# Attention's last 64 queries in one TensorE group for the scores and one for the values, and the last 64 keys as a block-diagonal tile

## The chip, the core and the metric

The kernel runs on one core of a Trainium2 chip. TensorE (PE) multiplies, VectorE (DVE) and ScalarE (ACT) work element by element, GpSimd (POOL) fills constants, and SyncE (SP) issues the transfers. The metric is the device time of one execution in microseconds. Every duration below comes from one profiled execution of the kernel before.

## The reference

Eight batches with eight heads of 576 tokens go through causal attention with a decay, and then through a two-layer network with a gate:

```python
B, H, S, D = 8, 8, 576, 64
cum    = cumsum(log(clip(f, 1e-4, 1)), -1)
scores = q @ k.T / sqrt(D) + cum[..., :, None] - cum[..., None, :]
scores = where(causal, -1e9, scores)
attn   = softmax(scores)                 # exp(scores - max), over the sum + 1e-9
x      = (attn @ v).transpose(0, 2, 1, 3).reshape(B * S, H * D)   # 4608 x 512
h      = x @ w_in                        # 512 -> 2048
g      = h * tanh(softplus(h))           # the Mish function
out    = g @ w_out                       # 2048 -> 512
```

## The kernel before

**Two streams of work.** Attention goes by pairs of heads: 32 pairs `g`, four to a batch. The network (`m1_items`, `m2_items`) goes by chunks of 512 tokens and 16 steps of 128 hidden units; eight chunks hold the first 512 tokens of a batch each, the ninth holds the last 64 tokens of all batches. Each float32 matrix is split into two float16 halves, so a product of the network is three matmuls of 512 columns: `b<-xa,wall` for the first layer, `b<-gh,wall` and `b<-gl,wall` for the second. ACT computes Mish (tile `me`), ACT or DVE makes its high half `gh` and DVE the low half `gl`.

**Order.** Nothing is issued as written. `Program.choose` collects every operation with its possible engines and a price, and `schedule` plays the program forward on priced engines (with nine backward passes for the ranks) and writes out the order with the earliest modelled end. Each engine then runs its list in that order, and semaphores hold it where an operand is late. An item given to `choose` as a list of several operations is placed as one piece: nothing is put between its parts. `beside` does that for products that fill half of the array each.

**Attention of pairs 4 to 31** (28 pairs; the first four go another way, which the change does not touch). Queries stand on the partitions. A pair's 576 queries are four blocks of 128 and a last one of 64, and the last 64 queries of both heads share one tile: head 0 on partitions 0 to 63, head 1 on 64 to 127. The functions are nested in `attn_moe`:

- `new_st_items` makes scores in a PSUM bank (two products each: 70 rows of `st`, then 128), finds the row's highest (`highest`, DVE), and takes exponentials (`exp`, ACT) into `st` (buffer `ST1[2]`); `turn` splits them into halves `hb` and transposes them by a transfer into `pt`. Its part `w_` is that of the last 64 queries: against the last 64 keys (bank `pv`, "narrow", 64 columns) and the first 512 (bank `ps`, "wide", 512 columns), for both heads: eight products `b<-st` that fill 64 of the array's 128 columns. The narrow exponentials go to `ev` (128x64), then twice side by side into `hv` (128x128), and by a transposing transfer into `tv`.
- `new_pv_items` multiplies exponentials by values (`b<-vv,pt`): `blocks` for whole query blocks, and `tail` for the last 64 queries: for four key blocks three products per head, 24 of half width, and for the last 64 keys three per head from `tv`, which take 64 rows and 64 columns of the array each (64*64 in the rows below).

Attention's PSUM banks are two (`bank`), taken in turn; the network has the other six. In ACT, exponentials and Mish need different tables, so that ACT_TABLE_LOAD stands wherever the order goes from one to the other.

The price of an operation on PE is (columns, active columns, half); a further product in one `choose` way cost 53 columns:

```python
if isinstance(cost, tuple) and total:
    total = (total[0] + 53, total[1] + cost[1], 0)
```

Of the kernel before, what the change touches and what calls it, by code (L numbers as in the profile page):

```python
# [15 lines left out]
F32 = mybir.dt.float32  # L16
# [10 lines left out]
P = 128  # L27
S = 576
# [30 lines left out]
NME = 5  # L59
NOT = 2  # L60
NGH = 5
SPD = 0
WO0 = 16
LWO = 4
# [77 lines left out]
class Program:  # L142
# [21 lines left out]
    def choose(self, *ways):  # L164

        r, w, opts = [], [], []
        for way in ways:
            total, port = 0.0, False
            for eng, method, a, kw in way:
                aps = [(k, x) for k, x in list(enumerate(a)) + list(kw.items()) if hasattr(x, "tensor")]  # L170
                w += [z for k, x in aps if k in ("out", "accum_out", 0) for z in self.region(x)]
                r += [z for k, x in aps if k not in ("out", "accum_out", 0) for z in self.region(x)]
                if eng == "scalar":
                    (r if method == "activation" else w).append(("table", 0, 1, 0, 1))
                if eng == "tensor":

                    w.append((w[0][0] + "/pe", 0, 1, 0, 1))
                port |= self.shared(eng, method, aps)
                cost = self.cost(eng, method, kw, aps)
                if isinstance(cost, tuple) and total:  # L180

                    total = (total[0] + 53, total[1] + cost[1], 0)
                else:
                    total = cost if isinstance(cost, tuple) else total + cost + (80 if total else 0)
            opts.append((eng, way, total, port))
        key = len(self.ops)
        if self.rank is not None:
            key, self.rank[1] = self.rank[0] + self.rank[1], self.rank[1] + self.rank[2]
        self.ops.append((opts, r, w, key))
        func = ways[0][0][3].get("func") if ways[0][0][0] == "scalar" and len(ways) == 1 else None  # L190
        self.sets.append("mish" if func == AF.Mish else "exp" if func == AF.Exp else None)

        self.banks.append({
            x.tensor.name for _, _, a, kw in ways[0] for x in list(a) + list(kw.values())
            if hasattr(x, "tensor") and x.space == PSUM})
# [361 lines left out]
def attn_moe(ctx: ExitStack, tc: tile.TileContext, qk, v, f, w_in, w_out, out):  # L557
# [325 lines left out]
    def bank(name, shape=(P, CH), dtype=F32):  # L883

        nonlocal nbank
        nbank += 1
        return psum(banks[nbank % len(banks)], shape, dtype)
# [227 lines left out]

    flat2 = ST1[2].rearrange("p j t s -> p (j t s)").bitcast(F32)
    ne = [0]

    def new_st_items(g):
        i = place1(g)  # L1120
# [62 lines left out]

        def w_():
            ps, pv = bank(f"sw_{g}"), bank(f"sv_{g}")
            for o, k in ((pv[:, 0:D], slice(CH, S)), (ps, slice(0, CH))):
                beside(*((
                    o[j * D : (j + 1) * D], q1[0 : KM - 1, j, CH:S], k1[0 : KM - 1, j, k], True, False)
                    for j in range(2)))
                beside(*((  # L1190
                    o[j * D : (j + 1) * D], q2[:, j, CH:S], k2[:, j, k], False, True) for j in range(2)))
            highest(pv[:, 0:D], 9, mskb2)
            highest(ps, 8, mskw[:, 0:1].to_broadcast([P, CH]), s["mx"][:, 9:10])
            ev = sp.tile([P, D], F32, name=f"ev{g}", tag="e4")
            exp(ev, pv[:, 0:D], 8)
            e = place_e()
            exp(e, ps, 8)

            h = sp.tile([P, 2, P], F16, name=f"hv{g}", tag="hv", bufs=1)
            t = sp.tile([P, 2, P], F16, name=f"tv{g}", tag="tv", bufs=2)  # L1200
            two = ev.unsqueeze(1).to_broadcast([P, 2, D])
            hh, ll = (h[:, i].rearrange("p (a d) -> p a d", a=2) for i in range(2))
            nc.choose(*(scaled(hh, two, None, x) for x in HW))
            nc.choose(*(sub(ll, two, hh, x) for x in LW_))
            nc.sync.dma_start_transpose(out=t, in_=h)
            s["V"] = t
            turn(e, "W")
# [5 lines left out]
    def new_pv_items(g):  # L1213
        b, p = divmod(g, NP)
        s = st[g]

        def products(o, t, k, c, vh, vl, first, last, r=slice(0, P)):
            n = 2 if s["V"] is t else 8
            hh, ll = t[r, k, c], t[r, n // 2 + k, c]
            return [(o, hh, vh, first, False), (o[:, 0:D], hh, vl, False, False), (o, ll, vh, False, last)]  # L1220

        def blocks(o, j, qt):
            name, k0 = ((f"Y{j}", 3), ("Z", 2 * j), (f"Y{j}", 0), (f"X{j}", 0))[qt]
            for kt in range(qt + 1):
                for a in products(
                        o, s[name], k0 + kt, slice(0, P), s["vh"][:, 2 * kt + j], s["vl"][:, 2 * kt + j],
                        kt == 0, kt == qt):
                    mm(*a)

        def tail(o):  # L1230
            for kt in range(5):
                both = []
                for j in range(2):
                    r = slice(j * D, (j + 1) * D)
                    if kt < 4:
                        both.append(products(
                            o[r], s["W"], kt, r, s["vh"][:, 2 * kt + j], s["vl"][:, 2 * kt + j], kt == 0, False))
                    else:
                        both.append(products(o[r], s["V"], 0, r, s["vh"][r, 8], s["vl"][r, 8], False, True, r))
                for x in zip(*both):  # L1240
                    beside(*x)

        def one(j):
            n = 4 + j
            o = bank(f"o{j}_{g}", (P, n, D + 1))
            for qt in range(4):
                blocks(o[:, qt], j, qt)
            if j:
                tail(o[:, 4])
            rr = sp.tile([P, 5], F32, name=f"rr{g}_{j}", tag="rr", bufs=4)[:, 0:n]  # L1250
            nc.vector.tensor_scalar(out=rr, in0=o[:, :, D], scalar1=1e-9, scalar2=None, op0=ALU.add)
            nc.vector.reciprocal(out=rr, in_=rr)
            if j == 0:
                s["x"] = sp.tile([P, 10, D], F32, name=f"x{g}", tag="x32", bufs=NX)
            nc.vector.tensor_tensor(
                out=s["x"][:, j:8:2], in0=o[:, 0:4, 0:D],
                in1=rr[:, 0:4].unsqueeze(2).to_broadcast([P, 4, D]), op=ALU.mult)
            if j:
                nc.vector.tensor_scalar(
                    out=s["x"][:, 8:10], in0=o[:, 4:5, 0:D].to_broadcast([P, 2, D]),  # L1260
                    scalar1=rr[:, 4:5], scalar2=None, op0=ALU.mult)

        return [(lambda: one(0), 40 * 30), (lambda: one(1), 45 * 30)]
# [374 lines left out]
```

## Time and profile before

| what | value |
|---|---|
| time, median of 3 runs | 1054.42 us (1052.96 to 1054.48) |
| time of the profiled execution | 1054.26 us |
| its span, first to last instruction | 1052.5 us |
| PE busy | 987.3 us (94%), 7214 matmuls |
| ACT busy | 779.1 us (74%), of it 259.2 us in 202 table loads |
| DVE busy | 733.5 us (70%) |
| POOL busy | 17.3 us (2%) |
| DMA | 146.80 MB, mean 139 GB/s |

The profiled execution lasted 1.8 us longer than its span; the difference lies around the instructions. In the profile a matmul's end is modelled: a product of 512 columns is listed with 0.38 us though the next starts some 0.215 us later. What PE's work costs is therefore read from the starts. Busy shares of one engine over the whole span mix stretches with different limits, so the rows below also give them by stretch.

### The profile page before, as it was taken

What the parts mean: (1) busy time and instruction counts of PE and PEld (TensorE: products, weight loads), DVE (VectorE), ACT (ScalarE), POOL (GpSimd) and SP (SyncE); (2) the same over time, 40 slices, a digit from 0 to 9 for tenths busy, and PEclk for the clock granted to TensorE, in tenths of its full rate; (3) what the DMA queues carried; (4) which work ended last, traced back from release to release, by engine and by line L of the source; (5) the groups of instructions that cost most, each with busy time, mean ns of one, the idle gap of its engine ahead of it and who ended that gap; (6) DMA issues with size and microseconds to landing.
All of it is one profiled execution on the core that took longest, in us unless ns stands there. A gap on an engine that the chain in (4) does not pass through costs nothing.

```text
span 1052.5 us, 19788 instructions
## 1 busy us (share of the span) xinstructions
PE 987.3 (94%) x7214; PEld 504.9 (48%) x7214; DVE 733.5 (70%) x2040; ACT 779.1 (74%) x1293; POOL 17.3 (2%) x59
## 2 busy tenths in 40 slices
PE   0599788999999999999999999999999999999998
PEld 0387344544445555554544554455544554444443
DVE  8989899998677787777777767787777653222221
ACT  5457899879799999898889989899989782112111
POOL 5000000000000000000000000000000000000000
PEclk9799988999999999999999999999999999999999
DMA  9888997877756766777566756775656432000001
GB/s 297 282 232 212 219 225 174 184 197 190 167 136 149 173 141 152 136 169 143 135 145 138 162 123 143 170 158 128 139 122 149 66 66 73 1 1 21 21 1 40
DMA packets 266258, 146.80 MB, mean 139 GB/s; under 512 B 233808, under 2 KB 234576, under 8 KB 266160
## 3 DMA queue, kind: packets, MB, share of 16 engines
q1 hardware_dynamic: 266160, 145.54, 59.0%
q8 instruction: 56, 0.92, 0.4%
q14 instruction: 42, 0.34, 0.1%
HBM read 48.37 MB, written 12.57 MB: 58 GB/s over the span
## 4 chain that ended last, share of the span: by engine, by line
PE 65%; DVE 13%; ACT 11%; DMA 7%; issue 3%; SPq 1%; ACTq 0%; DVEq 0%
PE b L290 65%; ACT L290 3%; DMA pt<-hb 3%; DVE b L290 2%; ACT st L290 2%; DVE wall L290 2%; ACT hb L290 2%; DVE hl L290 2%; DVE hb L290 2%; ACT junk L290 1%; DVE gl L290 1%; ACT me L290 1%; DMA wall<-in_w_in_dram 1%; DMA qk<-in_qk_dram 1%; DVE vv L290 1%
## 5 line engine op out<-in xcount | busy, mean ns | idle before, releaser
L290 PEld LDWEIGHTS <-wall 128*128 128x128 f16 x3456 | 331.7, 98 | 399.6 <-issue 22.4
L290 PE MATMUL b<-xa,wall 128*128 128x512 f16 x1728 | 418.1, 382 | 10.3 <-DVE wall L290 4.4
L290 PE MATMUL b<-gh,wall 128*128 128x512 f16 x1152 | 371.8, 380 | 0.1
L290 ACT ACT_TABLE_LOAD x202 | 259.2, 1283 | 6.6 <-DVE mn L290 2.6
L290 PE MATMUL b<-gl,wall 128*128 128x512 f16 x576 | 218.9, 380 | 0.0
L290 ACT ACTIVATE me<-b,cinv 128x512 f32<-128x512 f32 x144 | 98.8, 687 | 139.5 <-PE b L290 138.2
L290 DVE TENSOR_SCALAR gh<-me,gsc 128x512 f16<-128x512 f32 x125 | 60.3, 483 | 143.3 <-ACT me L290 142.6
L290 PE MATMUL b<-st 70*128 70x256 f16 (+11 forms) x888 | 139.0, 295 | 21.9 <-ACT st L290 5.2
L290 DVE TENSOR_TENSOR hb<-st,hb 128x512 f16<-128x512 f32 x168 | 114.3, 688 | 57.0 <-ACT hb L290 56.9
L290 ACT ACTIVATE st<-b,mn 128x512 f32<-128x512 f32 (+3 forms) x252 | 127.0, 541 | 34.4 <-DVE mn L290 29.6
L290 PE MATMUL b<-vv,pt 128*128 128x65 f16 (+5 forms) x2576 | 105.2, 202 | 5.6 <-ACT st L290 2.5
L290 DVE SCALAR_TENSOR_TENSOR gl<-me,gsc,gh 128x512 f16<-128x512 f32 x144 | 107.9, 750 | 3.5 <-ACT gh L290 0.3
L290 ACT ACTIVATE hb<-st 128x512 f16<-128x512 f32 x168 | 103.5, 628 | 6.6 <-DMA pt<-hb 5.5
L290 PEld LDWEIGHTS <-st 70*128 70x128 f16 (+3 forms) x888 | 67.6, 104 | 83.2 <-issue 46.0
L290 DVE CUSTOM_DVE_ANT_0 b<-b,mskw 128x512 f32<-128x512 f32 (+1 forms) x168 | 93.9, 565 | 17.6 <-PE b L290 15.1
L290 PEld LDWEIGHTS <-pt 128*128 128x128 f16 (+1 forms) x2352 | 72.5, 102 | 24.3 <-DMA pt<-hb 6.8
L290 DVE SCALAR_TENSOR_TENSOR hl<-qk,qt,hl 128x576 f16<-128x576 f32 x64 | 50.8, 810 | 0.7 <-ACT hl L290 0.7
L290 ACT ACTIVATE junk<-qk 128x576 bf16<-128x576 f32 x64 | 43.5, 679 | 5.9 <-DMA qk<-in_qk_dram 5.2
L290 DVE SCALAR_TENSOR_TENSOR wall<-wall 128x512 int32<-128x512 int32 x64 | 43.5, 686 | 0.1
L290 DVE DVE_READ_ACCUMULATOR2_ANT mn<- 128x1 f32 x280 | 39.8, 142 | 0.0
L290 DVE CUSTOM_DVE_ANT_0 b<-b,mskb 128x128 f32<-128x128 f32 (+1 forms) x84 | 23.6, 281 | 18.4 <-PE b L290 13.5
L290 ACT ACTIVATE junk<-wall 128x512 bf16<-128x512 f32 x32 | 20.1, 628 | 18.8 <-issue 10.5
(102 smaller groups left out, 605.2 us busy)
## 6 DMA issues: line engine op xcount, KB each, us to landing
st<-hl SPq DMA_DIRECT2D x192, 144.0 KB
qk<-in_qk_dram SPq DMA_DIRECT2D x32, 576.0 KB
v<-in_v_dram SPq DMA_DIRECT2D x32, 288.0 KB
out_dram<-ot SPq DMA_DIRECT2D x36, 256.0 KB
wall<-in_w_in_dram SPq DMA_DIRECT2D x16, 512.0 KB
wall<-in_w_out_dram SPq DMA_DIRECT2D x16, 512.0 KB
pt<-hb SPq DMA_TRANSPOSE x168
part<-ot SPq DMA_DIRECT2D x8, 256.0 KB
```

The source lines that it names most:

```text
L290: r = getattr(real[eng], method)(*a, **kw)
```

## The change

The eight score products of the last 64 queries become one `beside`, narrow before wide. The 24 half-width value products become one `beside`, too. The narrow exponentials are written into a 128x128 tile `evs` whose off-diagonal 64x64 blocks stay zero (two such tiles, filled with zeros once, used in turn); ACT writes the two diagonal blocks with one instruction each. The last 64 keys then take three whole-array products (128 rows, 128 columns) instead of six of 64*64. The planner's price of a group is now 480 columns and, for each product, half of its columns and 20.

```diff
+SWITCH = 480
@@ choose
-                if isinstance(cost, tuple) and total:
-                    total = (total[0] + 53, total[1] + cost[1], 0)
+                if isinstance(cost, tuple) and len(way) > 1:
+                    n, active = total or (SWITCH, 0.0, 0)[:2]
+                    total = n + 0.5 * cost[0] + 20, active + cost[1]
                 else:
                     total = cost if isinstance(cost, tuple) else total + cost + (80 if total else 0)
+            if isinstance(total, tuple) and len(way) > 1:
+                total = (*total, 0)
@@ ahead of new_st_items
+    evs = cp.tile([P, 2, P], F32, name="evs")
+    nc.gpsimd.memset(evs.rearrange("p a n -> p (a n)"), 0.0)
@@ w_
+            both = []
             for o, k in ((pv[:, 0:D], slice(CH, S)), (ps, slice(0, CH))):
-                beside(*((
+                both += [(
                     o[j * D : (j + 1) * D], q1[0 : KM - 1, j, CH:S], k1[0 : KM - 1, j, k], True, False)
-                    for j in range(2)))
-                beside(*((
-                    o[j * D : (j + 1) * D], q2[:, j, CH:S], k2[:, j, k], False, True) for j in range(2)))
+                    for j in range(2)]
+                both += [(
+                    o[j * D : (j + 1) * D], q2[:, j, CH:S], k2[:, j, k], False, True) for j in range(2)]
+            beside(*both)
-            ev = sp.tile([P, D], F32, name=f"ev{g}", tag="e4")
-            exp(ev, pv[:, 0:D], 8)
+            ev = evs[:, g % 2]
+            for j in range(2):
+                r = slice(j * D, (j + 1) * D)
+                nc.scalar.activation(
+                    out=ev[r, r], in_=pv[r, 0:D], func=AF.Exp, scale=-1.0, bias=s["mx"][r, 8:9])
-            two = ev.unsqueeze(1).to_broadcast([P, 2, D])
-            hh, ll = (h[:, i].rearrange("p (a d) -> p a d", a=2) for i in range(2))
-            nc.choose(*(scaled(hh, two, None, x) for x in HW))
-            nc.choose(*(sub(ll, two, hh, x) for x in LW_))
+            nc.choose(*(scaled(h[:, 0], ev, None, x) for x in HW))
+            nc.choose(*(sub(h[:, 1], ev, h[:, 0], x) for x in LW_))
@@ tail
-            for kt in range(5):
-                both = []
-                for j in range(2):
-                    r = slice(j * D, (j + 1) * D)
-                    if kt < 4:
-                        both.append(products(
-                            o[r], s["W"], kt, r, s["vh"][:, 2 * kt + j], s["vl"][:, 2 * kt + j], kt == 0, False))
-                    else:
-                        both.append(products(o[r], s["V"], 0, r, s["vh"][r, 8], s["vl"][r, 8], False, True, r))
-                for x in zip(*both):
-                    beside(*x)
+            both = []
+            for kt in range(4):
+                for x in zip(*(products(
+                        o[r], s["W"], kt, r, s["vh"][:, 2 * kt + j], s["vl"][:, 2 * kt + j], kt == 0, False)
+                        for j, r in enumerate((slice(0, D), slice(D, P))))):
+                    both += x
+            beside(*both)
+            for a in products(o, s["V"], 0, slice(0, P), s["vh"][:, 8], s["vl"][:, 8], False, True):
+                mm(*a)
```

The planner writes a new order from this, on every engine. Three places show it; buffer numbers are one higher after the change, because of the new tile.

PE, scores of the last queries of one pair in the middle of the kernel. Before, the narrow group (`b_0_115`, 64x64) stands by itself among products of the network; the pair's wide group stands 18 rows earlier, after other products of the network:

```order
L290 MATMUL b_0_119<-gl_169,wall 128x512
L290 LDWEIGHTS st_0_82
L290 MATMUL b_0_115<-st_0_82 64x64
L290 LDWEIGHTS st_0_82
L290 MATMUL b_0_115<-st_0_82 64x64
L290 LDWEIGHTS st_1_86
L290 MATMUL b_0_115<-st_1_86 64x64
L290 LDWEIGHTS st_1_86
L290 MATMUL b_0_115<-st_1_86 64x64
L290 LDWEIGHTS wall
L290 MATMUL b_0_119<-gh_168,wall 128x512
```

The same pair after the change, from the last narrow product on:

```order
L293 LDWEIGHTS st_1_86
L293 MATMUL b_0_116<-st_1_86 64x64
L293 LDWEIGHTS st_0_82
L293 MATMUL b_0_125<-st_0_82 64x512
L293 LDWEIGHTS st_0_82
L293 MATMUL b_0_125<-st_0_82 64x512
L293 LDWEIGHTS st_1_86
L293 MATMUL b_0_125<-st_1_86 64x512
L293 LDWEIGHTS st_1_86
L293 MATMUL b_0_125<-st_1_86 64x512
L293 LDWEIGHTS wall
L293 MATMUL b_0_120<-gh_169,wall 128x512
```

The wide products have moved to the narrow ones' place, right behind them. In the whole order before, 26 narrow groups of the 28 pairs stand alone, 21 wide groups stand alone as four, one stands right behind a pair's values, four pairs' wide groups are cut in two by other work, and two pairs have all eight together; after, all 28 stand as eight.

PE, the end of one pair's values. Before, the six products of the last 64 keys (`tv`) are of 64 output columns:

```order
L290 MATMUL b_0_115<-vv_128,pt_135 64x65
L290 LDWEIGHTS tv_165
L290 MATMUL b_0_115<-vv_128,tv_165 64x65
L290 LDWEIGHTS tv_165
L290 MATMUL b_0_115<-vv_128,tv_165 64x65
L290 LDWEIGHTS tv_165
L290 MATMUL b_0_115<-vv_128,tv_165 64x64
L290 LDWEIGHTS tv_165
L290 MATMUL b_0_115<-vv_128,tv_165 64x64
L290 LDWEIGHTS tv_165
L290 MATMUL b_0_115<-vv_128,tv_165 64x65
L290 LDWEIGHTS tv_165
```

The same pair after the change:

```order
L293 LDWEIGHTS pt_136
L293 MATMUL b_0_116<-vv_129,pt_136 64x65
L293 LDWEIGHTS tv_166
L293 MATMUL b_0_116<-vv_129,tv_166 128x65
L293 LDWEIGHTS tv_166
L293 MATMUL b_0_116<-vv_129,tv_166 128x64
L293 LDWEIGHTS tv_166
L293 MATMUL b_0_116<-vv_129,tv_166 128x65
L293 LDWEIGHTS st_0_82
L293 MATMUL b_0_125<-st_0_82 128x384
```

Six products of 64 output rows have become three of 128, at the same place: behind the 24 of half width.

ACT, from the 13th Mish of the kernel (`me`) on. Before, three follow each other under one table load:

```order
L290 ACT_TABLE_LOAD
L290 ACTIVATE me_173<-b_0_117,cinv_96 128x512
L290 ACTIVATE hb_163<-st_2_84 128x512
L290 ACTIVATE gh_174<-me_173,gsc_100 128x512
L290 ACTIVATE wall<-wall,wsc 128x512
L290 ACTIVATE me_176<-b_0_118,cinv_96 128x512
L290 ACTIVATE xp_0_152<-x_0_147 128x512
L290 ACTIVATE gh_177<-me_176,gsc_100 128x512
L290 ACTIVATE xp_0_153<-x_0_147 128x128
L290 ACTIVATE wall<-wall,wsc 128x512
L290 ACTIVATE me_180<-b_0_117,cinv_96 128x512
```

After the change, from the same Mish (`me_174`) on, exponentials (`st_2_84`) stand between them, with a table load each way:

```order
L293 ACT_TABLE_LOAD
L293 ACTIVATE me_174<-b_0_118,cinv_96 128x512
L293 ACTIVATE hb_164<-st_2_84 128x512
L293 ACT_TABLE_LOAD
L293 ACTIVATE st_2_84<-b_0_116,mn_167 128x512
L293 ACT_TABLE_LOAD
L293 ACTIVATE me_177<-b_0_119,cinv_96 128x512
L293 ACTIVATE hb_163<-st_2_84 128x512
L293 ACT_TABLE_LOAD
L293 ACTIVATE st_2_84<-b_0_116,mn_167 128x384
L293 ACTIVATE st_2_84<-b_0_116,mn_167 128x128
L293 ACTIVATE gh_178<-me_177,gsc_100 128x512
```

Up to the 12th Mish the order has 17 of these loads before and 19 after, up to the 20th 29 and 35, and in all 202 and 204. The narrow exponentials are 28 ACT instructions before and 56 after.

## Rows read from the trace of the kernel before

**Rows 1.** The profile's page: the span, and busy time (share of the span, instructions) of each engine.

```profile
span 1052.5 us, 19788 instructions
PE 987.3 (94%) x7214; PEld 504.9 (48%) x7214; DVE 733.5 (70%) x2040; ACT 779.1 (74%) x1293; POOL 17.3 (2%) x59
```

**Rows 2.** Busy time by stretch: the stretch from the span's start and its length, then busy us (instructions) of each engine, the granted clock of TensorE, the DMA engines' share and rate.

```profile
core 0: us, PE busy (x) PEld busy (x) DVE busy (x) ACT busy (x) POOL busy (x), PEclk, DMA share, GB/s
...
100.00:150.00 50.00, 38.53 (x272) 18.39 (x271) 46.64 (x137) 46.43 (x90) 0.14 (x1) 0.92 1.06 233
150.00:193.00 43.00, 37.97 (x303) 19.30 (x301) 41.22 (x123) 41.70 (x80) 0.28 (x2) 0.86 0.83 185
193.00:230.00 37.00, 36.37 (x257) 17.79 (x256) 36.82 (x108) 27.69 (x49) 0.14 (x1) 1.00 0.80 193
230.00:262.00 32.00, 30.36 (x229) 15.10 (x228) 28.46 (x91) 30.01 (x51) 0.14 (x1) 1.00 0.72 186
...
300.00:400.00 100.00, 99.85 (x785) 50.06 (x784) 77.60 (x224) 92.93 (x147) 0.55 (x4) 1.00 0.66 152
...
700.00:800.00 100.00, 99.79 (x808) 50.77 (x807) 78.58 (x226) 93.09 (x141) 0.55 (x4) 1.00 0.59 132
...
875.00:1052.50 177.50, 173.68 (x805) 78.56 (x803) 42.69 (x73) 32.02 (x49) 0.00 (x0) 1.00 0.06 20
```

**Rows 3.** The four largest of the waits of PE between 200 and 875 us: what it waited for, us in total, times, the longest.

```profile
PE b L290 <- ACT st L290: 1.8, 5, 0.6
PE b L290 <- DVE x L290: 1.8, 2, 1.4
PE b L290 <- ACT me L290: 1.3, 1, 1.3
PE b L290 <- ACT e L290: 1.1, 1, 1.1
```

**Rows 4.** PE in order of time round one narrow group: start and length in us, the product with rows*columns of the array, columns streamed, and how many.

```profile
392.75 0.38 PE L290 MATMUL b<-gh,wall 128*128 128x512 f16 x1
393.05 0.25 PE L290 MATMUL b<-st 70*64 70x64 f16 x4
393.24 0.39 PE L290 MATMUL b<-gh,wall 128*128 128x512 f16 x1
```

**Rows 5.** The same view round one wide group that stands alone.

```profile
769.63 0.59 PE L290 MATMUL b<-gh,wall 128*128 128x512 f16 x2
770.16 0.62 PE L290 MATMUL b<-st 70*64 70x512 f16 x4
770.71 0.39 PE L290 MATMUL b<-gl,wall 128*128 128x512 f16 x1
```

**Rows 6.** The same view where one half of a cut wide group stands alone: the first row is one whole product of 256 columns and the two wide half-array products of 512 columns behind it.

```profile
796.76 0.61 PE L290 MATMUL b<-st 128*128 128x256 f16 x3
797.30 0.39 PE L290 MATMUL b<-gh,wall 128*128 128x512 f16 x1
```

**Rows 7.** The same view at one of the two pairs whose eight score products stand together already.

```profile
825.86 0.38 PE L290 MATMUL b<-gh,wall 128*128 128x512 f16 x1
826.17 0.69 PE L290 MATMUL b<-st 70*64 70x64 f16 x8
826.79 0.39 PE L290 MATMUL b<-xa,wall 128*128 128x512 f16 x1
```

**Rows 8.** The same view at the end of one pair's values: the first row is the last whole product and the 24 of half width behind it, the second the six of 64*64.

```profile
741.12 0.69 PE L290 MATMUL b<-vv,pt 128*128 128x65 f16 x25
741.75 0.28 PE L290 MATMUL b<-vv,tv 64*64 64x65 f16 x6
741.96 0.39 PE L290 MATMUL b<-xa,wall 128*128 128x512 f16 x1
```

**Rows 9.** The same view at three whole value products (of 65, 65 and 64 columns) that are issued right behind a half-array group.

```profile
579.71 0.27 PE L290 MATMUL b<-vv,pt 128*128 128x65 f16 x3
```

**Rows 10.** PE's groups of instructions by shape: count, busy us, mean ns of one, and idle us of PE just before them with what ended it.

```profile
L290 PE MATMUL b<-st 70*64 70x512 f16 x56 | 11.4, 401 | 0.7 <-ACT st L290 0.7
L290 PE MATMUL b<-st 70*64 70x64 f16 x56 | 6.1, 215 | 1.1 <-ACT st L290 1.1
```

**Rows 11.** DVE in order of time where it reads one pair's narrow and then wide scores (`b<-b,mskb 128x64` and `b<-b,mskw,mn 128x512`), the idle time before the first in brackets.

```profile
749.72 0.23 DVE L290 CUSTOM_DVE_ANT_0 b<-b,mskb 128x64 f32<-128x64 f32 x1 [1.70 <-PE b L290]
...
750.05 0.76 DVE L290 CUSTOM_DVE_ANT_0 b<-b,mskw,mn 128x512 f32<-128x512 f32 x1
```

**Rows 12.** PE in order of time where that pair's wide group (x4) was issued, the idle time of PE before it in brackets.

```profile
742.56 0.62 PE L290 MATMUL b<-st 70*64 70x512 f16 x4 [0.21 <-ACT st L290]
```

**Rows 13.** ACT in order of time round one narrow exponential (`e`).

```profile
753.67 0.30 ACT L290 ACTIVATE e<-b,mn 128x64 f32<-128x64 f32 x1
753.87 0.63 ACT L290 ACTIVATE hb<-st 128x512 f16<-128x512 f32 x1
```

**Rows 14.** ACT's groups by shape between 193 and 262 us: count, busy us, mean ns of one, idle us before them.

```profile
L290 ACT ACT_TABLE_LOAD x14 | 18.0, 1283 | 1.1 <-DVE rr L290 0.5 <-DVE mn L290 0.4
...
L290 ACT ACTIVATE me<-b,cinv 128x512 f32<-128x512 f32 x9 | 6.2, 685 | 0.1
```

**Rows 15.** POOL in order of time: the last constant that it fills without a wait, and the next one.

```profile
12.86 0.48 POOL L290 MEMSET mskw<- 128x384 bf16 x1
21.32 0.77 POOL L290 COPY mskw<-mskb 128x128 bf16<-128x128 bf16 x1 [7.97 <-DVE mskb L290]
```

More of the change, by code (lines that the diff above doesn't have):

```diff
@@ L1215, in new_pv_items, with products @@
         s = st[g]
-        def products(o, t, k, c, vh, vl, first, last, r=slice(0, P)):
+        def products(o, t, k, c, vh, vl, first, last):
             n = 2 if s["V"] is t else 8
-            hh, ll = t[r, k, c], t[r, n // 2 + k, c]
+            hh, ll = t[:, k, c], t[:, n // 2 + k, c]
             return [(o, hh, vh, first, False), (o[:, 0:D], hh, vl, False, False), (o, ll, vh, False, last)]
```

## The prediction, made before the changed kernel ran

> **What bounds the kernel now.** I began with the page's busy times: PE leads with 94% [rows 1]. A share over the whole span can hide stretches with another limit, so the table by stretches came next [rows 2]. There the reader is to see two regimes. From 300 us on PE is busy for 99.85 and 99.79 of 100 us in the two stretches shown, while ACT has some 7 us of each hundred left and DVE over 20. Between 100 and 193 us PE is busy for only 38.53 + 37.97 = 76.5 of 93 us; DVE (87.9) and ACT (88.1) are full there, and a shorter group on PE gives nothing back. From 193 us PE is back at 36.4 of 37. Then I asked what PE waits for between 200 and 875 us, where nearly all of attention of this form runs: the four largest causes come to 6.0 us in all [rows 3]. So behind the first 200 us the end moves with the sum of what PE executes, and the question is what the changed groups cost in PE's own time.
>
> **The cost of the score groups.** Busy time doesn't tell this, since half-array products lie on top of each other; I take the start of the first product behind a group, less the moment at which it would have started had the group not been there. Two products of the network listed in one row last 0.59 us and one 0.38 [rows 4, 5], so one takes 0.21 to 0.22, say 0.215.
> - Narrow alone: the next starts at 393.24, due at 392.75 + 0.215, so 0.275 us [rows 4].
> - Wide alone: 770.71, due at 769.63 + 0.43, so 0.65 us [rows 5].
> - One half of a wide group cut in two: 797.30, due at 796.76 + 0.11 (256 columns), so 0.43 us [rows 6]. Two halves cost 0.86, 0.21 more than a whole.
> - All eight together: 826.79, due at 825.86 + 0.215, so 0.715 us [rows 7].
>
> The trace thus holds the new form of the scores already. A pair saves 0.65 + 0.275 - 0.715 = 0.21 us, and 28 pairs 5.9. The order adds four cut groups (4 x 0.21 = 0.84), takes away the two pairs that stand together already (0.42) and some 0.1 each where two wide pieces adjoin a pair's values: 6.1 us.
>
> **The cost of the values.** From the last whole product to the work behind it the group takes 741.96 - 741.12 = 0.84 us, and the six products of 64*64 have 0.21 of it, 741.75 to 741.96 [rows 8]. The three whole products have no row of their own (`tv` as a whole array). The nearest is three whole value products behind a half-array group, of the same columns: listed with 0.27 us in all [rows 9], and with 0.19 for the modelled rest of the last the third starts some 0.075 us after the first; a slot more for itself, 0.03, makes 0.105 us. The first whole product has to wait for the array as the first of the six does, so I leave that moment where it is. Saving: 0.21 - 0.105 = 0.105 us a pair, 2.9 us over 28. Bounds: 0.21 us (the three cost nothing more) and 0 (they cost as much as six), 5.9 and 0 us over the kernel. I take the middle, since the row it comes from has the same shapes behind the same kind of group. The 24 products of half width were adjacent before and are still.
>
> **What of it counts.** 6.1 + 2.9 = 9.0 us of PE's time, 0.32 us a pair. Some three pairs fall into 100 to 193 us, where PE idles anyway: 3 x 0.32 = 0.95 us is lost. That leaves 8.05 us.
>
> **What the switches are worth, by the skill.** Eight together cost 0.715 where wide alone costs 0.65: the narrow four are worth 0.065 us among others of their kind, and 0.275 by themselves. Going into and out of half-array form thus costs 0.21 us here [rows 4, 5, 7]. The Trainium skill, "TensorEngine Tiling (Array Packing)", section "Tiling Modes", says that changing the tiling mode drains TensorE, and changing the tile alone does not; the trace agrees in kind. It gives no figure there; "TensorE: Matmul & The Clock Gate", section "Single matmul latency", has 398 cycles around a product that isn't hidden in a stream, 0.166 us at 2.4 GHz. By that figure, as an estimate, in and out would be 0.33 us and the saving of this change some 14 us; the measured 0.21 decides.
>
> **ACT and the rest.** One narrow exponential keeps ACT from the next instruction for 753.87 - 753.67 = 0.20 us [rows 13]. There are 28 more of them: 5.6 us, by the 0.30 us of its listed length 8.4 at most, and nothing if half the partitions took half the time. They lie in ACT's free 7 us of each hundred [rows 2]; without that cover they would be added in full. The order also has six table loads more up to the 20th Mish, 6 x 1.283 = 7.7 us of ACT, and only two more at the end. Between 193 and 262 us, where nine Mish and 14 loads run [rows 14], ACT has 37 - 27.69 + 32 - 30.01 = 11.3 us free [rows 2]. I take 0 for it and keep 7.7 as the other end. Filling `evs` falls into the 7.97 us that POOL waits at 13.3 us; a fill of 384 bf16 columns took 0.48 us there [rows 15], so this one costs nothing, and about that if it were not covered.
>
> **What is delayed.** The wide scores now go out with the narrow ones, later than before. DVE reads a pair's wide scores at 750.05, behind its narrow ones at 749.72 [rows 11], though PE had issued the wide group at 742.56 [rows 12]: the early start only held a bank. The narrow scores in turn are ready when all eight are done at the latest, 0.715 - 0.275 = 0.44 us later. DVE waited 1.70 us for them already, and behind them stand the pair's exponentials on ACT and the next score block's bank; PE has products of the network for that time. I take 0, and the price without cover is 28 x 0.44 = 12.3 us.
>
> **The sum.** 1054.26 us, the profiled execution's own time, less 8.05 is 1046.2 us. The median of the runs stands 0.16 above that execution. I say **1046 us**.
>
> **The rivals.**
> - *The gain goes under in table loads* (chance 0.12): between 193 and 262 us the six loads are not covered, since exponentials come back late for PE's value products. PE waits for `st` longest among its waits today [rows 3]. Price up to 7.7 us: 1053.9 us, no change. Against it: 11.3 us free on ACT, and DVE, not ACT, is full up to 230 us [rows 2].
> - *Slower, the wait for two banks* (0.06): one group of eight needs the banks of both score blocks at once, and PE's queue stands still if one isn't read out. Today a wide group waited 0.21 us for ACT, and nothing of PE's came in between [rows 12]. (The Trainium skill, "PSUM — Partial Sum Buffer", section "Engine vs sequencer instructions", says that matmuls start in program order; the trace agrees with that 0.21 us.) From (8.05 + 2.1) / 28 = 0.36 us a pair on, the kernel is slower by over 0.2%. At 0.6 us, PE's longest wait for `st` [rows 3], it ends at 1046.2 + 16.8 = 1063 us. Against it: both groups' waits together are 0.7 + 1.1 = 1.8 us over 28 pairs, 0.06 each [rows 10].
> - *More is won, the order fits better* (0.12): the old price made narrow and wide (4 x 53 + 2 x 64 + 2 x 512 columns at 2.4 GHz, 0.57 us) cheaper than the 0.925 read above; the new one (480 + 4 x 276 + 4 x 52 columns, 0.75 us) is near 0.715. If PE's 6.0 us of waits [rows 3] vanish with it, 1040 us. Against it: a new order is a new draw, and most of these waits are single ones.
> - *A switch costs more than the groups read here tell* (0.03): a network product is listed with 0.38 us though it takes 0.215, so 0.165 us of it lie hidden [rows 4]. If each switch bared all of that, scores save 28 x 0.33 = 9.2 and values, with one switch fewer, 28 x 0.165 = 4.6 us; less three pairs, 1041.7 us. This is what the figure of 0.166 us in the skill's section "Single matmul latency" (of "TensorE: Matmul & The Clock Gate") would make of it. The group of eight in the trace speaks against it.
>
> **Chances and range.** The forecast itself, PE's saving with a new order's usual scatter, has 0.67, between 1043 and 1050 us. About 0.2% (2.1 us) is what a measurement of this kernel can tell from no change. Faster than that: nearly all of the forecast, and the third and fourth rival, 0.80. Same: the first rival and a little of the forecast, 0.13. Slower: the second and what a worse start may add, 0.07. Below 1040 lies half of the third rival (0.06), above 1053 half of the first and the second (0.12): range 1040 to 1053.
>
> **What would show it.** In the new trace: 28 rows of eight score products that cost 0.71 us each by the starts round them; from the first `tv` product to the next work 0.10 to 0.12 us instead of 0.21; half-array instructions of 64*64 from `tv` gone; 28 more narrow exponentials, and ACT still some per cent below full between 300 and 800 us; PE's busy time in those stretches unchanged near 100%. I would be wrong if PE's busy share between 193 and 300 us fell by several us, if `PE b <- ACT st` or a wait for DVE in front of the group of eight grew to ten us and more, or if the groups took longer than read here.

## The result, and the profile after

The change made the kernel slower: 1064.95 us in the median (1062.76 to 1065.88, 4 runs) beside 1054.45 for the kernel before in the same session. The ratio is 1.0097 (95% interval 1.0083 to 1.0110), so 10.2 us were lost where 8 were to be won. Ratios below are made the same way, against runs of the kernel before beside each kernel; a ratio is not the quotient of the two medians, and the two can differ by 0.1%.

The head of the page for the kernel after, as [rows 1]:

```profile
span 1064.0 us, 19681 instructions
PE 985.0 (93%) x7130; PEld 502.4 (47%) x7130; DVE 732.6 (69%) x2040; ACT 793.3 (75%) x1323; POOL 17.6 (2%) x60
```

The table by stretches, columns as in [rows 2]:

```profile
core 0: us, PE busy (x) PEld busy (x) DVE busy (x) ACT busy (x) POOL busy (x), PEclk, DMA share, GB/s
100.00:150.00 50.00, 39.55 (x259) 18.72 (x257) 47.71 (x137) 41.94 (x79) 0.14 (x1) 0.90 0.89 208
150.00:193.00 43.00, 32.63 (x291) 17.07 (x288) 38.10 (x112) 39.78 (x75) 0.28 (x2) 0.88 0.80 175
193.00:230.00 37.00, 33.95 (x247) 16.54 (x246) 35.23 (x101) 34.06 (x57) 0.14 (x1) 1.00 0.80 192
230.00:262.00 32.00, 31.20 (x230) 15.43 (x229) 28.13 (x90) 30.72 (x52) 0.46 (x1) 1.00 0.81 189
300.00:400.00 100.00, 98.11 (x786) 49.84 (x785) 74.58 (x212) 90.88 (x144) 0.55 (x4) 1.00 0.65 145
700.00:800.00 100.00, 98.31 (x741) 48.75 (x740) 75.14 (x222) 92.58 (x143) 0.42 (x3) 1.00 0.58 128
```

In the two stretches of 100 us PE is down from 99.85 and 99.79 to 98.11 and 98.31, and ACT is no busier than before. No engine has become full; PE waits more, for these (200 to 875 us: what it waited for, us in total, times, the longest):

```profile
PE b L293 <- ACT st L293: 5.8, 12, 1.0
PE b L293 <- DVE x L293: 4.7, 8, 1.3
PE b L293 <- ACT me L293: 2.1, 2, 1.5
PE b L293 <- ACT evs L293: 1.7, 4, 0.7
```

That is 14.3 us beside the 6.0 of [rows 3]. The list names only waits that the trace can put down to somebody. More of PE's lost time can be estimated from its starts: from one product on all 128 columns of the array to the next product, less the time its columns take at the granted clock of 1.00 (0.215 us for 512), counted where more than 0.1 us is left over. Between 200 and 900 us this sum is 13.4 us before and 31.0 after. It is called PE's lost time below.

PE's own work did shrink as forecast. The eight score products, in order of time:

```profile
730.03 0.81 PE L293 MATMUL b<-xa,wall 128*128 128x512 f16 x3
730.77 0.69 PE L293 MATMUL b<-st 70*64 70x64 f16 x8
731.39 0.39 PE L293 MATMUL b<-xa,wall 128*128 128x512 f16 x1
```

The next product starts at 731.39, due at 730.03 + 3 x 0.215 = 730.675: 0.715 us. The end of one pair's values:

```profile
752.64 0.27 PE L293 MATMUL b<-vv,tv 128*128 128x65 f16 x3
752.75 0.38 PE L293 MATMUL b<-xa,wall 128*128 128x512 f16 x1
```

From the first `tv` product to the next work it takes 0.11 us, where [rows 8] have 0.21. What did not come out is on ACT, where the narrow exponentials are now two (in order of time, `x2` is the pair):

```profile
736.91 0.62 ACT L293 ACTIVATE evs<-b,mn 64x64 f32<-64x64 f32 x2
737.55 0.63 ACT L293 ACTIVATE hb<-st 128x512 f16<-128x512 f32 x1
```

They keep ACT from the next instruction for 737.55 - 736.91 = 0.64 us; the one of [rows 13] took 0.20. The extra is 0.44 us a pair and 12.3 us over 28, not 5.6.

### The profile page after: what moved, and what is told of

Its sections match the earlier page's. It is cut to its first block, busy times and chain, and to the rows that moved or that the text cites. A ratio compares the mean times of both kernels' runs of the same rounds, so it can differ in the third digit from the quotient of the medians.

```text
span 1064.0 us, 19681 instructions
## 1 busy us (share of the span) xinstructions
PE 985.0 (93%) x7130; PEld 502.4 (47%) x7130; DVE 732.6 (69%) x2040; ACT 793.3 (75%) x1323; POOL 17.6 (2%) x60
## 4 chain that ended last, share of the span: by engine, by line
PE 37%; ACT 23%; DVE 11%; issue 6%; DMA 6%; SPq 1%; ACTq 0%; DVEq 0%
PE b L293 37%; ACT L293 8%; ACT st L293 4%; ACT hb L293 3%; ACT me L293 3%; DVE b L293 2%; ACT junk L293 2%; DMA pt<-hb 2%; DMA st<-hl 2%; DVE hb L293 2%; DVE gl L293 2%; DMA qk<-in_qk_dram 1%; ACT xa L293 1%; DVE gh L293 1%; SPq L293 1%
## 5 line engine op out<-in xcount | busy, mean ns | idle before, releaser
L293 PE MATMUL b<-st 70*128 70x256 f16 (+11 forms) x888 | 135.7, 292 | 31.6 <-ACT st L293 8.4
L293 ACT ACTIVATE junk<-qk 128x576 bf16<-128x576 f32 x64 | 43.5, 680 | 11.8 <-DMA qk<-in_qk_dram 11.0
L293 DVE TENSOR_SCALAR rr<-b 128x4 f32<-128x4 f32 (+1 forms) x64 | 10.2, 160 | 31.6 <-PE b L293 22.6
```

The lines of the kernel that those rows point to most:

```text
L293: r = getattr(real[eng], method)(*a, **kw)
```

## The experiments

The expectations name theories by a letter. **R**: TensorE alone paces the kernel behind 200 us (the prediction). **A**: ACT paces. **B**: ACT and TensorE, with orders fixed, hold each other up, so that a saving or a load on either counts in part. **P**: the new price of groups makes a worse order. **G**: a group of eight waits for two banks. **D**: any new order is a draw, and this one was a bad one. "Held" means that the planner was given the old prices for the edited operations, so that the order stays that of the kernel before but for a few rows. "Shaken" means that a small random number (`NZ = 3`) was added to each rank, with another seed, which gives a new order of the same operations. In the held runs PE, ACT and DVE list what they list before in the same order, the edited rows apart; only the last of them (one exponential) also has one row moved from DVE to ACT and a few on DVE. The lines that set the old prices are left out of the diffs.

**Two exponentials alone.** The kernel before, with only its narrow exponential cut in two; the products on PE stay as they were. First with a new order, then held:

```diff
-            exp(ev, pv[:, 0:D], 8)
+            for j in range(2):
+                r = slice(j * D, (j + 1) * D)
+                nc.scalar.activation(
+                    out=ev[r], in_=pv[r, 0:D], func=AF.Exp, scale=-1.0, bias=s["mx"][r, 8:9])
```

> The kernel before, with one edit: each pair's narrow exponential is taken by two ACT instructions of 64 partitions instead of one of 128; TensorE's groups, tiles and prices as before. Theory A (ACT sets the pace: in the changed kernel the two halves lie behind each other without overlap, 0.31 + 0.33 us from start to start, where the one before held ACT for 0.20, so about 0.44 us a pair or 12 us over 28 pairs, and little of it is covered): 1061 to 1067 us. Theory P (the new price makes the order worse) and theory G (the group of eight delays the score blocks): no change, 1052 to 1057 us. Theory D (any new order scatters by several us): anything from 1050 to 1062.

> The kernel before with each engine's order held as it was (the two half exponentials are one item at the price of the one); ACT's instruction for the narrow exponential becomes two of 64 partitions, 12 us more of ACT over 28 pairs, nothing else. Theory R (TensorE alone paces the kernel, ACT's free 7 to 10% take up what is added): 1053 to 1056 us. Theory A (ACT paces it): 1060 to 1067. Theory B (both are bound to each other in an order that has no play left: a part of what is added shows): 1057 to 1060.

Measured: 1059.4 us, ratio 1.0055 (1.0034 to 1.0076), with the new order, in the range of D alone; 1061.29, 1.0072 (1.0053 to 1.0091), held. PE's lost time is 23.0 and 20.0 us. So 5 to 8 us, half of the loss or more, come with ACT's second instruction alone. In the held run, where nothing else differs, 6.7 / 12.3 = 54% of what was put on ACT shows by the medians, and 7.6 us, 62%, by the ratio. R falls; 1061.29 lies in the range named for A, 1.3 us above that for B, so this run alone doesn't tell these two apart.

**One exponential in the change.** ACT makes one tile of 128x64, and DVE copies its halves into `evs`:

```diff
+            e0 = sp.tile([P, D], F32, name=f"ev{g}", tag="e4")
+            exp(e0, pv[:, 0:D], 8)
             for j in range(2):
                 r = slice(j * D, (j + 1) * D)
-                nc.scalar.activation(
-                    out=ev[r, r], in_=pv[r, 0:D], func=AF.Exp, scale=-1.0, bias=s["mx"][r, 8:9])
+                nc.vector.tensor_copy(out=ev[r, r], in_=e0[r])
```

> The changed kernel, with one edit: one ACT instruction of 128 partitions takes the narrow exponential into a 128x64 tile, and two DVE copies put its halves into the diagonal blocks; groups, price and whole-array products as in the change. Theory A: ACT gets some 0.44 us a pair back, and TensorE's saving of 8 us shows: 1044 to 1051 us. Theories P and G: as the change, 1062 to 1067 us. Theory D: between.

Measured: 1057.61, 1.0033 (1.0019 to 1.0048), 7 us below the change and between the ranges of A and of P and G, as D had it. It points the same way, but its order is new, and the shaken runs below show that orders alone differ by nearly as much.

**How much of a saving on PE shows.** Before's order held, and a quarter of the columns of every `b<-gl,wall` left out, or most columns of the square sums of q and k on ACT:

```diff
-                mm(o, wh, gl[:, 0:n], False, False)
+                mm(o[:, 0:384], wh, gl[:, 0:384], False, False)
```

```diff
-            square_sum(am[:, j : j + 1], x[:, j])
+            square_sum(am[:, j : j + 1], x[:, j, 0:D])
```

> The kernel before with each engine's order held; the 576 products of the low halves in the second layer stream 384 of 512 columns, 576 x 0.053 = 31 us less TensorE, about 14 of it behind 875 us where attention is over and TensorE works alone. It leaves out a quarter of those products. Theory R: all of it shows, 1022 to 1027 us. Theory A: the part behind 875 us alone, 1038 to 1042. Theory B: between, 1028 to 1037.

> The kernel before with each engine's order held; the square sums of q and k are taken over 64 of 576 columns, some 0.4 us less ACT for each of 64, 27 us in all. It leaves out most of those sums. Theory R: 1053 to 1055 us. Theory A: 1030 to 1040. Theory B: 1046 to 1052.

Measured: 1041.6 us, 0.9888 (0.9860 to 0.9917), with less on PE; 1050.98, 0.9972 (0.9957 to 0.9988), with less on ACT. The second run takes ACT's 64 square sums from 43.5 to 16.1 us of busy time, and of these 27 us only 3.0 (by the ratio) to 3.6 (by the medians) show: A falls. The first run tells most about PE. The products it shortens that lie behind attention (from 867.7 us on, count and busy time), PE's `tv` products of the whole span with the start of the first and the last, in the kernel before (L290) and here, and two stretches:

```profile
L291 PE MATMUL b<-gl,wall 128*128 128x384 f16 x140 | 45.6, 326 | 0.0
```

```profile
L290 PE MATMUL b<-vv,tv x168: 189/193/214, 131.5 to 874.6; 64*64 64x65 f16 x112, 64*64 64x64 f16 x56
L291 PE MATMUL b<-vv,tv x168: 189/193/214, 129.1 to 867.5; 64*64 64x65 f16 x112, 64*64 64x64 f16 x56
```

```profile
300.00:400.00 100.00, 97.99 (x798) 50.66 (x797) 76.41 (x222) 93.30 (x148) 0.56 (x4) 1.00 0.67 152
700.00:800.00 100.00, 97.90 (x810) 50.82 (x809) 78.24 (x227) 92.80 (x144) 0.55 (x4) 1.00 0.62 133
```

A shortened product saves 128 columns, a quarter of 0.215 us. The 140 behind attention save 7.5 us, and the time from the last `tv` product to the end of the span fell by 7.6 (before 1052.5 - 874.6 = 177.9, here 1037.8 - 867.5 = 170.3): there everything shows. The 436 ahead of that save 23.4 us, and the last `tv` product moved from 874.6 to 867.5: 7.1 us, 30%. That is an upper bound: the first `tv` product already came 2.4 us earlier, with six shortened products (0.3 us) ahead of it, and the profiled execution, 1039.62 us, is 2 us below the run's median. The medians leave 1054.58 - 1041.6 - 7.5 = 5.5 us, 23%, and the ratio 11.8 - 7.5 = 4.3, 18%. So a fifth to a quarter of the saving shows during attention. The rest became waiting (lost time 31.2 us beside 13.4):

```profile
PE b L291 <- ACT st L291: 8.7, 21, 0.9
PE b L291 <- DVE x L291: 3.7, 8, 1.8
PE b L291 <- DMA pt<-hb: 2.9, 3, 1.3
PE b L291 <- ACT me L291: 2.8, 2, 1.5
```

R falls here too. So does A once more: by A only the 7.5 us behind attention would show, 1047 us (the range named for it, 1038 to 1042, took some 14 us to lie there). What is left is B: a lighter PE runs into the engines that feed it. The page's chain of work that ended last (followed back from the last instruction, each step to what released it) has changed accordingly. Before, then here:

```profile
PE 65%; DVE 13%; ACT 11%; DMA 7%; issue 3%; SPq 1%; ACTq 0%; DVEq 0%
PE 36%; ACT 26%; DVE 22%; issue 8%; DMA 7%; SPq 1%; ACTq 0%; DVEq 0%
```

That PE was 99.8% busy because the order was planned for all of these engines at one pace is the likely reason, but no run shows it.

**The block-diagonal tile alone.** Before's order held, `evs` with two exponentials, and three whole `tv` products in the place of six. Then the same tile from one exponential: DVE, which masks the narrow scores in any case, writes them twice side by side, with -2^115 off the diagonal, and one exponential of 128x128 gives the blocks and their zeros.

```diff
-            highest(pv[:, 0:D], 9, mskb2)
+            pd = pv[:, P : 2 * P].rearrange("p (a d) -> p a d", a=2)
+            nc.vector.tensor_tensor_reduce(
+                out=pd, in0=pv[:, 0:D].unsqueeze(1).to_broadcast([P, 2, D]), in1=mskd,
+                scale=-0.125, scalar=3e38, op0=ALU.add, op1=ALU.min, accum_out=s["mx"][:, 9:10])
...
+            exp(ev, pv[:, P : 2 * P], 8)
```

> The kernel before with each engine's order held; the last 64 keys go as in the change: two half exponentials into the diagonal blocks of the zeroed tile (ACT 12 us more) and three whole-array products instead of six of 64*64 (TensorE 3 us less), scores and the other values as before. Theory R: 1050 to 1053 us. Theory A: 1060 to 1067, as h1_held_two_exps. Theory B: 1054 to 1058.

> Before's order held, as in the held block-diagonal run: the values of the last keys are three whole-array products, and the only difference to that run is how the block-diagonal tile comes about. DVE writes the narrow masked scores twice into 128 columns (a mask of -2^115 off the diagonal), so that one exponential of 128x128 on ACT makes the whole tile: 28 exponentials instead of 56. B (ACT and TensorE bound to each other, so that ACT's 0.44 us a pair counts for about half): some 6 us less than the held block-diagonal run's 1057.1, so 1050 to 1052.5 us, below the kernel before. A (ACT alone paces): 1055 us minus at most 1. Were ACT's halves not the cause: 1056 to 1058 us.

Measured: 1057.08, 1.0026 (1.0015 to 1.0037), with two; 1052.19, 0.9981 (0.9972 to 0.9991), with one; both as B had it. ACT in order of time round the one:

```profile
754.39 0.36 ACT L291 ACTIVATE e<-b,mn 128x128 f32<-128x128 f32 x1
754.64 0.63 ACT L291 ACTIVATE hb<-st 128x512 f16<-128x512 f32 x1
```

It holds ACT for 0.25 us instead of 0.64. Over 28 pairs 10.9 us less on ACT are worth 4.9 us of time, 45%, in nearly the same order. Beside the held run with two exponentials and six products (1061.29) the three whole products won 4.2 us, which is no less than the 2.9 us they save on PE. That is more than the fifth to a quarter above: what share of a saving shows depends on where it is made and is no constant of the kernel. So this part of the change is good by itself, and is faster than the kernel before once ACT isn't made to pay for it.

**The scores alone, the price, and the draw.** The kernel before with the eight scores as one group, at the old price; the whole change at the old price; and before and after shaken with two seeds (shown: the old price in the change, and the first seed):

```diff
-                    n, active = total or (SWITCH, 0.0, 0)[:2]
-                    total = n + 0.5 * cost[0] + 20, active + cost[1]
+                    n, active, k = total or (0.0, 0.0, 0)
+                    total = n + (53 if k % 2 else cost[0]), active + cost[1], k + 1
```

```diff
-SEED = 122
-NZ = 0
+SEED = 1
+NZ = 3
```

> The kernel before, with the eight score products as one group and nothing else of the change (values, exponential and price of a pair as before). Theory A: TensorE saves 6 us and ACT's work stays: 1046 to 1051 us. Theory G: the group waits for two banks, 1058 us or more. Theory P: no price is changed, so as theory A. Theory D: 1046 to 1058.

> Only the group of eight score products, old price, with the order shaken once (ranks disturbed as in the shaken runs before). If the 3 us that this part won without shaking are its own and not a lucky order: 1049 to 1053 us. D (luck): 1054 us and more.

> The changed kernel, with one edit: the planner's price of a group is again the sum over its pairs as before the change (a pair's columns and 53), without the 480 columns of the switch; the work of every engine is that of the change. Theory P: the loss goes, 1045 to 1055 us. Theories A and G: 1061 to 1067 us. Theory D: anything from 1055 to 1070.

> The kernel before, with its planner's first ranks shaken by random numbers below 3 (one draw): the same work in another order. Theory D (a new order by itself scatters by several us, and the order before was a lucky one): 1057 us or more. Theories A and P (what costs is ACT's extra work, or the price): within 3 us of the kernel before, 1051 to 1057.

> The changed kernel, with its first ranks shaken the same way. Theory D: between 1050 and 1065, 5 us or more from the change. Theories A and P: within 3 us of the change, 1062 to 1068.

> As d1_before, a second draw. Theory D: 1057 us or more, and several us from the first draw. Theories A and P: 1051 to 1057.

> As d1_after, a second draw. Theory D: 1050 to 1065, several us from the first draw. Theories A and P: 1062 to 1068.

Measured: the scores alone 0.9968 (0.9955 to 0.9981), but shaken 1.0007 (0.9993 to 1.0021): the 3 us won were at least in part an order's luck, and this part is worth 1 us on the mean of the two. Before, shaken: 1.0008 (0.9990 to 1.0026) and 1.0018 (1.0004 to 1.0032). After, shaken: 1.0048 (1.0028 to 1.0068) and 1.0039 (1.0022 to 1.0056). So all three orders of the change stand above all three of before. Between those shaken alike the difference is 4 us with the first seed and 2 with the second, where the intervals overlap; the order that the change got is 5 to 6 us worse than its other two. The shaken change, 1057 to 1058 us, lies in the range of D and below that of A and P. The change at the old price: 1.0023 (1.0007 to 1.0039), no proof of P next to those.

**Both causes taken apart.** The change with the tile from one exponential (the edit above), at the new and at the old price, each also shaken with one seed:

> The change, with its new price, but the block-diagonal tile from one exponential of 128x128 (DVE writes the masked narrow scores in two halves, off the diagonal -2^115). The order is drawn anew. B: the change's orders drawn otherwise gave 1057.0 and 1058.4 us; less some 5 us for ACT 1052 to 1054 us. P (the new price orders the work worse): 1057 us and more, since the price is kept. D: anything up to 1065 us.

> The same with the old price of a pair of half-array products. B: 1050 to 1054 us, like the run with the new price within 2 us. P: 5 us and more below that run. The local sum (8 us of TensorE saved, nothing lost on ACT) would give 1046 us.

> The change with the block-diagonal tile from one exponential of 128x128, new price, and the order shaken with the same disturbed ranks as the first shaken pair. The shaken change stood at 1.0048 of the kernel before, the shaken kernel before at 1.0008. B: some 5 us less than the shaken change, 0.998 to 1.001 (1052 to 1055 us). P or D: 1.003 and more (1057 us).

> The same with the old price of the groups, and the same disturbed ranks. If the price itself costs: 2 to 7 us less than the run beside it. If not: within 2 us of it, either way. If the form wins for good, below 1052.5 us (0.998).

Ratios of all the orders of the full change, unshaken first:

| the tile `evs` from | new price | old price |
|---|---|---|
| two exponentials of 64x64 | 1.0097, 1.0048, 1.0039 | 1.0023 |
| one of 128x128 | 1.0001, 1.0030 | 0.9984, 0.9961 |

(The intervals of the lower row: 0.9987 to 1.0016, 1.0019 to 1.0042, 0.9966 to 1.0001, 0.9942 to 0.9980.) The means are 1.0061, 1.0023, 1.0016 and 0.9973. From the upper to the lower row they fall by 4.6 and 5.0 thousandths: some 5 us for ACT's second exponential, as in the held runs. From the left to the right column they fall by 3.8 and 4.3: some 4 us for the price. The first is borne out by two pairs of runs with the order held; the second rests on means over one to three orders. Three pairs of runs differ in the price alone, and with it in their order: with two exponentials the ratio fell by 0.0074 and with one by 0.0017, where the intervals meet, and by 0.0069. The shaken run with one exponential at the new price missed the range that B gave it (0.998 to 1.001) and lies where P or D had put it. Of the forms with the whole products from `tv` two beat both kernels: the shaken one at the old price, 1048.59 us, and the held one, 1052.19.

## Why the prediction was wrong

**What held.** The groups cost what was read: 0.715 us for eight scores and 0.11 for the three whole products, so PE's work did fall by some 9 us. All 23 groups of eight that nothing held up cost 0.713 to 0.716 us. Filling `evs` fell where POOL had time:

```profile
12.97 0.31 POOL L293 MEMSET evs<- 128x256 f32 x1
19.81 0.78 POOL L293 COPY mskw<-mskb 128x128 bf16<-128x128 bf16 x1 [6.53 <-DVE mskb L293]
```

**The step that failed first: "So behind the first 200 us the end moves with the sum of what PE executes".** It was read off PE's 99.8% [rows 2] and the 6.0 us of its waits [rows 3]. Both say that PE waits little at PE's present length; neither says what happens when PE gets shorter. By the held run with shorter products a fifth to a quarter of a saving shows during attention, which would have made 1.5 to 2 us of the 8.05; the change with neither ACT's second exponential nor the new price won 2.8 us on the mean of two orders (0.9973).

**The second: ACT's exponentials at nothing.** The size was off, 12.3 us instead of 5.6, past even the bound of 8.4. The forecast priced an extra instruction by the 0.20 us at which an instruction on 128 partitions is followed by another; two on half of the partitions each take 0.64 us together. And the cover failed: "ACT's free 7 us of each hundred" were gaps in which ACT waited for an operand, not time in hand. Of its 43.9 idle us between 300 and 800 us before, most end with the rows' highest from DVE (`mn`), the largest part this:

```profile
ACT st L290 <- DVE mn L290: 21.3, 20, 2.3
```

Between 300 and 800 us both kernels take the narrow exponentials of 18 pairs, and ACT is no busier after (454.7 us beside 456.1): that order has 141 table loads there instead of 146. About half of an added ACT microsecond ends up in the time: 5 us here. (Of ACT time taken away from the square sums only 11 to 13% came back, so the half holds for this place.)

**The third, not foreseen: the order.** "A new order is a new draw" was mentioned for the gain and not for the loss. At the new price the orders are some 4 us slower than at the old. It is nearer to the measured cost of a score group (0.75 us for 0.715, where the old makes 0.57), but farther from that of the 24 value products: 480 + 16 x 52.5 + 8 x 52 = 1736 columns, 0.73 us, where they take 0.60 ([rows 8]: 741.75 - 741.12, less 0.03 for the whole product) and the old price makes 8 x 118 + 4 x 117 = 1412 columns, 0.59. Whether that is why is open. The order that the change got is another 4 us worse than the mean of its three (1.0097 beside 1.0061). Together: -2.8 for PE, +5 for ACT, +4 for the price and +4 for this order make the 10.2 us measured. All four are read from one table, so that they add up proves nothing; the first is near the 1.5 to 2 us by the held run with shorter products, the second agrees with the held exponentials, and the last two come from few orders and are the soft ones.

**The rivals.** The wait for two banks (G), the only one on the slow side, isn't the cause. The scores alone as groups of eight were not slower (0.9968 and 1.0007), and in the change PE's waits right ahead of a group of eight are 1.3 us over 28 groups, 0.83 of them in one place:

```profile
569.01 0.69 PE L293 MATMUL b<-st 70*64 70x64 f16 x8 [0.83 <-ACT st L293]
```

The table loads don't explain the loss, but part of it does lie at the start. There are 17 loads between 193 and 262 us, where [rows 14] have 14, and PE's busy time there is 33.95 + 31.20 = 65.15 us beside 66.73 [rows 2]; between 100 and 193 us it is 72.2 beside 76.5. By 300 us PE has started 585 of the network's products, 597 before, and 607 and 609 in the change's two shaken orders. These 22 to 24 products, some 5 us, are about what this order is worse than the other two, so the bad luck of this order lies ahead of 300 us. But the shaken order with 607 has 37 loads up to the 20th Mish, the change 35; what in its order held the change up is open. A better order did not come, and a dearer switch than the groups show didn't either. Of the signs that were to tell against the forecast, PE's busy time between 193 and 300 us fell by 2.1 us (102.4 to 100.3), and its wait for `st` grew, from 1.8 to 5.8 us, but most of that was not in front of the group of eight.

## What to carry to other kernels

A busy share near 100% shows that an engine is full, not that it alone sets the pace: where an order is planned for several engines at once, test with one shortened instruction type how much of a saving shows before summing it, and expect a load on the next-fullest engine to show in part as well. Price an added instruction by the starts of two in a row of the same shape on the same partitions, and its cover by what that engine could have done in its gaps. And where an edit redraws the order, compare several orders of both kernels, since the draw alone was worth 5 to 6 us here, half of what the change lost.

## What the runs showed of the hardware

Cutting an ACT instruction by partitions tripled its cost, while doubling its columns added a quarter: 0.20 us for 128x64, 0.25 for 128x128, 0.64 for two of 64x64. The reason is an overlap that halves don't get. One of the two places in the kernel after where something came between the halves (ACT in order of time; the first `evs` is the lower half of the partitions, the second the upper):

```profile
173.66 0.69 ACT L293 ACTIVATE st<-b,mn 128x512 f32<-128x512 f32 x1
174.25 0.30 ACT L293 ACTIVATE evs<-b,mn 64x64 f32<-64x64 f32 x1
174.44 0.62 ACT L293 ACTIVATE hb<-st 128x512 f16<-128x512 f32 x1
175.09 0.31 ACT L293 ACTIVATE evs<-b,mn 64x64 f32<-64x64 f32 x1
175.41 1.28 ACT L293 ACT_TABLE_LOAD   x1
```

The lower half starts 0.10 us ahead of its predecessor's end (173.66 + 0.69 = 174.35), and its successor starts 0.11 ahead of its own; the upper half starts 0.03 behind `hb`'s end. In the other 26 pairs the halves are neighbours, and the second never starts before the first has ended. The Trainium skill, "ScalarE: Activation LUTs", section "What ACT_TABLE_LOAD costs", says that back-to-back instructions overlap by some 0.093 us. This trace agrees for most neighbours on all partitions (391 of 440 overlap, by 0.10 us in the median) and where the lower half is next to one on all (0.10 to 0.11 us), and not where the upper half comes first or second.
